# Opening of a fused FFT-and-gating kernel: loads of x and stores of turned weights moved into the next phase, bias rows sorted between its steps

## The chip, the cores and the metric

One core of one Trainium2 chip. The metric is device time in microseconds (us). Times from a trace are counted from the start of the profiled span, which is about 1.8 us shorter than the time of the same run. Engines: PE multiplies matrices, ACT (ScalarE) and DVE (VectorE) work on elements, POOL and SP here mostly issue DMAs; `bk` in a line is one of the banks that PE writes its results to. The granted clock is the share of PE's full clock that it was given, 1.00 for all of it; "half clock" below is a granted clock of 0.50.

## The reference

```python
X = fft(fft(x, axis=1), axis=2).real                # x: 8 x 3072 x 256
h = maximum(X @ w_in, 0)                            # 256 -> 1024
u, v = h[..., :512], h[..., 512:]
v_n = (v - mean(v)) / sqrt(var(v) + 1e-6)           # over the last axis
v_s = einsum('ts,bsd->btd', w_spatial, v_n) + b_spatial[None, :, None]
out = (u * v_s) @ w_out                             # 8 x 3072 x 256
```

`w_spatial` is 3072 x 3072. The kernel turns its rows on PE (transposes), keeps the turned rows on chip for the first batch and stores them in DRAM (`rawd`) for later batches. `b_spatial` has to be brought into the order in which the kernel makes its output rows.

## The kernel before

The opening makes the tables, folds x of batch 0 and turns the first three weight rows. Then comes V of batch 0: twelve tiles in a pipeline of steps t = 0, 1, 2, ... Each tile has two matmul halves, a root and a normalisation, so tile n has its root at step n + 2. ACT and DVE share this work, and the turning of weight rows 3 to 5 goes on in steps 1 to 9. After V the kernel goes through chunks of output until the end.

The bias rows go through this code. They are copied with strides into the fp32 columns 0 to 4607 of `regf`, a difference is added, and one store brings them to DRAM:

```python
def bias_sort():
    for src, so_, st, do_, ds in ((0, 0, 2, 0, 1152), (0, 1, 2, 2304, 1536),
                                  (1, 0, 2, 384, 1152), (1, 3, -2, 2688, 768)):
        DVE.tensor_copy(out=view(regf, do_, [[ds, 2], [1, 384]], 1),
                        in_=view(bsrc[src], so_, [[st, 2], [4, 384]], 1))
    rows = lambda k: view(regf, 384 * k, [[1152, 4], [1, 384]], 1)
    tt(DVE, rows(2), rows(0), rows(1), SUB)
    SP.dma_start(out=dram(bprm, 0, ...), in_=view(regf, 0, [[1, 4608]], 1))
```

`regf` is `reg` seen as fp32. Normalised V of batch 0 is written into `reg` from its first byte on: for tile 0 DVE writes the fp32 columns 0 to 255 and ACT the columns 3072 to 3327. Both lie within the sorted rows, so these must have been read out before V is written.

The opening and the loop of V, cut:

```python
prep_x(1, 0)                    # x of batch 1: SP loads it, POOL loads its mirror image
POOL.dma_start(out=wob, ...)    # w_out
...
prep_x(1, 1, homes[1])

def keep(i):                    # stores turned row i
    ACT.dma_start(out=dram(rawd, ...), in_=view(reg, ...))

def turning(i, on_dve=(1,)):    # three turn steps of row i; behind the last of them:
    def last(g=ts[-1]):
        g()
        keep(i)
        ...                     # the next weight loads by POOL
t0, t1, t2 = [turning(i, ()) for i in range(3)]
...
prep_x(1, 2, homes[2])
...
bias_sort()
load_bias(0)
for st in transform_steps(0, 0): st()
...
for t in range(len(pipes) + 5):
    if 5 <= t: first_products(*order[t - 5])
    for k in (3, 2, 1, 0):      # norm of tile t-3, root of t-2, second half of t-1, first half of t
        if 0 <= t - k < len(pipes): pipes[t - k][k]()
    for st in extra.get(t, ()): st()
    if 1 <= t < 10: ts[t - 1]()  # turning rows 3 to 5
    if 9 <= t < 17: us[t - 9]()
```

## Time and profile before

| | before |
|---|---|
| median of 6 runs (lowest to highest) | 1298.28 us (1296.81 to 1299.16) |
| span of the profiled run | 1295.2 us |
| PE busy | 96% of the span |
| ACT's first turn copy of V, and its first root | 48.28 and 50.61 us |
| ACT's first normalisation | 52.61 us |
| PE's last run of twelve matmuls of V's products before chunk 0 | 87.43 us |

PE is busy nearly throughout, so a change of the opening acts through *when* each later piece starts. I therefore follow one number through this text, the **lead**: how much earlier the same instruction starts than in the profiled run of the kernel before. The landmarks are ACT's root instructions (one for each tile of V) and, later, its copies of the output; at the end it is the difference of the spans.

### The profile page before, as it was taken

Reading aid. Unit: us, or ns where it says so; the run is one execution under the profiler, and the core shown is the slowest. Engines: PE = TensorE matmul, PEld = TensorE weight load, DVE = VectorE, ACT = ScalarE, POOL = GpSimd, SP = SyncE. Lnnn points to the kernel's source line nnn. Section 1 sums busy time; section 2 is a strip of 40 time slices with the busy share of each in tenths; the row PEclk is TensorE's granted clock in tenths of the full one; section 3 lists DMA queues with packets and bytes.
Section 4 is the critical chain, followed back from the end, with each engine's and each line's share of the span. In section 5 each row is a group of like instructions: output and inputs, shape, how many; then the busy total and the mean of one; then the engine's idle time right before and its main releaser. Section 6 shows DMA issues by size and latency. Waiting matters only on the chain.

```text
span 1295.2 us, 20931 instructions
## 1 busy us (share of the span) xinstructions
PE 1240.7 (96%) x8056; PEld 764.7 (59%) x8056; DVE 763.5 (59%) x1580; ACT 677.8 (52%) x1508; POOL 269.8 (21%) x318
## 2 busy tenths in 40 slices
PE   3689989999999999999999999999999999999998
PEld 2356555655666566665666666665666666666665
DVE  8677325446866846666555746666555744446333
ACT  8663767645554455555555455565555455551111
POOL 7101101002221222222121212222211112222222
PEclk9899999999999999999999999999999999999999
DMA  9949888576698878887788878887788778778885
GB/s 218 253 98 253 193 189 200 176 268 264 253 352 330 296 283 284 298 279 285 260 289 284 292 265 294 286 282 285 262 294 281 266 260 286 266 279 305 299 305 196
DMA packets 101442, 343.54 MB, mean 265 GB/s; under 512 B 7611, under 2 KB 57307, under 8 KB 77789
## 3 DMA queue, kind: packets, MB, share of 16 engines
q1 hardware_dynamic: 43902, 248.61, 54.0%
q0 software_dynamic: 25312, 49.55, 17.0%
q10 hardware_dynamic: 32128, 44.05, 9.6%
q8 instruction: 63, 1.03, 0.3%
q14 instruction: 37, 0.30, 0.1%
HBM read 300.46 MB, written 67.66 MB: 284 GB/s over the span
## 4 chain that ended last, share of the span: by engine, by line
PE 75%; issue 9%; ACT 6%; DVE 4%; POOL 3%; DMA 3%; ACTq 0%; POOLq 0%; DVEq 0%
PE bk L115 73%; POOL sumd L1011 2%; ACT reg L664 2%; PE bk L657 2%; DMA ovl<-in_moe_w_spatial_dram 1%; ACT junk L474 1%; ACT reg L488 1%; DMA sumd<-ovl 1%; DVE u L165 1%; DMA reg<-in_x_dram 1%; POOL reg L165 1%; DVE oto L165 1%; DVE xst L165 1%; DVE y L165 1%; ACT vt L466 0%
## 5 line engine op out<-in xcount | busy, mean ns | idle before, releaser
L115 PE MATMUL bk<-reg 128*128 128x384 bf16 (+1 forms) x5576 | 980.5, 326 | 8.3 <-ACT reg L664 3.6
L115 PEld LDWEIGHTS <-reg 128*128 128x128 bf16 x5576 | 541.9, 98 | 370.6 <-issue 16.1
L599 ACT COPY ost<-bk 128x512 f32<-128x512 f32 (+1 forms) x128 | 61.2, 480 | 251.6 <-PE bk L115 233.9
L165 POOL TENSOR_TENSOR p<-y,qt 128x384 f32<-128x384 f32 x48 | 62.7, 1307 | 545.0 <-DVE y L165 545.0
L488 ACT ACTIVATE reg<-vt,sm 128x512 bf16<-128x512 f32 x168 | 127.5, 806 | 46.7 <-DVE sm L165 44.4
L165 DVE TENSOR_TENSOR u<-y,u 128x384 bf16<-128x384 f32 x256 | 143.5, 561 | 10.1 <-ACT ost L599 0.5
L474 ACT ACTIVATE junk<-vt,sm 128x512 bf16<-128x512 f32 x168 | 121.3, 722 | 46.1 <-DVE sm L468 33.0
L165 DVE TENSOR_TENSOR y<-bk,bias 128x384 f32<-128x384 f32 x160 | 88.6, 554 | 80.9 <-PE bk L115 79.9
L115 PE MATMUL bk<-wob,u 128*128 128x256 bf16 x768 | 100.5, 273 | 0.2 <-ACT ost L599 0.2
L165 DVE TENSOR_TENSOR qt<-qt,bk 128x384 f32<-128x384 f32 x48 | 26.6, 554 | 124.0 <-PE bk L115 124.0
L580 ACT ACTIVATE u<-bk 128x384 bf16<-128x384 f32 x128 | 61.7, 482 | 67.1 <-PE bk L115 67.1
L574 ACT ACTIVATE u<-bk 128x384 bf16<-128x384 f32 x128 | 61.2, 478 | 50.8 <-PE bk L115 50.8
L115 PEld LDWEIGHTS <-u 128*128 128x128 bf16 x768 | 75.1, 98 | 19.6 <-DVE u L165 0.4
L165 POOL TENSOR_TENSOR qt<-y,qt 128x384 f32<-128x384 f32 x48 | 62.6, 1305 | 53.4 <-DVE y L165 53.0
L165 DVE TENSOR_TENSOR ovl<-reg 128x1536 bf16<-128x1536 bf16 x60 | 56.7, 952 | 23.6 <-DMA reg<-rawd 9.1
L453 ACT ACTIVATE vt<-bk 128x512 f32<-128x512 f32 x84 | 49.7, 591 | 35.1 <-PE bk L115 34.7
L468 DVE TENSOR_SCALAR sm<-sm 128x2 f32<-128x2 f32 x84 | 32.4, 386 | 55.5 <-ACT vt L466 54.5
L165 DVE TENSOR_TENSOR reg<-reg 128x3072 bf16<-128x3072 bf16 (+3 forms) x39 | 63.5, 1629 | 0.2
L466 ACT ACTIVATE vt<-bk 128x512 f32<-128x512 f32 x84 | 49.1, 584 | 27.8 <-PE bk L115 27.6
L1011 POOL DMA_DIRECT2D sumd<-ovl x60 | 32.6, 543 | 139.8 <-DVE ovl L165 129.1
L165 DVE TENSOR_TENSOR qt<-bias,bk 128x384 f32<-128x384 f32 x48 | 26.6, 553 | 59.5 <-PE bk L115 59.5
L165 POOL TENSOR_TENSOR p<-p,y 128x384 f32<-128x384 f32 x48 | 47.8, 996 | 59.2 <-DVE y L886 38.6
(144 smaller groups left out, 1258.1 us busy)
## 6 DMA issues: line engine op xcount, KB each, us to landing
reg<-sumd SPq DMA_DIRECT2D x120, 1152.0 KB
reg<-rawd SPq DMA_DIRECT2D x64, 1152.0 KB
out_dram<-ost ACTq DMA_DIRECT2D x64, 384.0 KB
sumd<-ovl POOLq DMA_DIRECT2D x60, 384.0 KB, 4.5
rawd<-reg ACTq DMA_DIRECT2D x24, 768.0 KB
bias<-bprm SPq DMA_DIRECT2D x32, 576.0 KB
ovl<-in_moe_w_spatial_dram POOLq DMA_DIRECT2D x34, 384.0 KB, 8.8
xst<-in_x_dram SPq DMA_DIRECT2D x20, 512.0 KB
```

What stands on the lines that cost most here:

```text
L115: PE.matmul(o, lhsT=l, rhs=r, start=start, stop=stop, skip_group_check=True)
L165: eng.tensor_tensor(out=o, in0=a, in1=b_, op=op)
L453: ACT.activation(out=v, in_=bk, func=AF.Relu, accum_out=sm[:, 0:1])
L466: ACT.activation(out=v, in_=bk, func=AF.Relu, accum_out=sm[:, 1:2])
L468: DVE.tensor_scalar(out=sm[:, 2:4], in0=sm[:, 0:2], scalar1=-1.0 / DH, scalar2=None, op0=MUL)
L474: ACT.activation(out=junk, in_=s["v%d" % i], func=AF.Square, bias=sm[:, 2 + i:3 + i], accum_out=sm[:, 4 + i:5 + i])
L488: ACT.activation(out=v_out(b, i, t), in_=v_in(b, s["v%d" % i]), func=AF.Identity, scale=sm[:, 6 + i:7 + i], bias=sm[:, 8 + i:9 + i])
L574: ACT.activation(out=u[:, jc, 0, :], in_=src, func=AF.Relu)
L580: ACT.activation(out=u[:, jc, 1, :], in_=src, func=AF.Relu)
L599: ACT.copy(out=s["o"][:, rs[0]:rs[0] + len(rs), :], in_=view(bk, 0, [[256, len(rs)], [1, 256]]))
L657: PE.transpose(bk[:, 128 * n:128 * n + 128], view(src, off, [[4, 128]]), idn)
L1011: POOL.dma_start(out=sumd[c, mi][:, 1536 * r:1536 * r + 1536], in_=o)
```

## The change

Its intent: take out of the opening what is not wanted there. x of batch 1 and the first stores go into the steps of V, where DMA is less busy, and the bias rows are sorted in gaps of DVE.

```diff
-        for src, so_, st, do_, ds in (...four copies...):
+        def copy(src, so_, st, do_, ds):
             DVE.tensor_copy(...)
-        rows = ...
-        tt(DVE, rows(2), rows(0), rows(1), SUB)
-        SP.dma_start(out=dram(bprm, ...), in_=view(regf, 0, [[1, 4608]], 1))
+        def diff():
+            rows = ...
+            tt(DVE, rows(2), rows(0), rows(1), SUB)
+            SP.dma_start(out=dram(bprm, ...), in_=view(regf, 0, [[1, 4608]], 1))
+            load_bias(0)
+        return [...the four copies...] + [diff]
...
-    prep_x(1, 0)
...
-    prep_x(1, 1, homes[1])
...
-    def turning(i, on_dve=(1,)):
+    def turning(i, on_dve=(1,), kept=True):
...
-            keep(i)
+            if kept:
+                keep(i)
...
-    t0, t1, t2 = [turning(i, ()) for i in range(3)]
+    t0, t1, t2 = [turning(i, (), False) for i in range(3)]
...
-    prep_x(1, 2, homes[2])
-    bias_sort()
-    load_bias(0)
...
-        ts += turning(i)
+        ts += turning(i, (1,), False)
+    later = {t: [] for t in range(len(pipes) + 5)}
+    for t, st in zip((0, 0, 1, 1, 2), bias_sort()):
+        later[t].append(st)
+    for j, t in enumerate((5, 8, 11)):
+        later[t].append(lambda j=j: prep_x(1, j, homes[j]))
+    for i, t in enumerate((7, 9, 10, 12, 14, 15)):
+        later[t].append(lambda i=i: keep(i))
...
-            for st in extra.get(t, ()):
+            for st in extra.get(t, []) + later[t]:
```

The stores of rows 3 to 5 move too.

More of the change, by code (lines that the diff above doesn't have):

```diff
@@ L378, in bias_sort @@
     def bias_sort():
-        for src, so_, st, do_, ds in ((0, 0, 2, 0, 1152), (0, 1, 2, 2304, 1536),
-                                      (1, 0, 2, 384, 1152), (1, 3, -2, 2688, 768)):
+        def copy(src, so_, st, do_, ds):
             DVE.tensor_copy(out=view(regf, do_, [[ds, 2], [1, 384]], 1),
                             in_=view(bsrc[src], so_, [[st, 2], [4, 384]], 1))
-        rows = lambda k: view(regf, 384 * k, [[1152, 4], [1, 384]], 1)
-        tt(DVE, rows(2), rows(0), rows(1), SUB)
-        SP.dma_start(out=dram(bprm, 0, [[4608, 1], [1, 4608]]),
-                     in_=view(regf, 0, [[1, 4608]], 1))
+        def diff():
+            rows = lambda k: view(regf, 384 * k, [[1152, 4], [1, 384]], 1)
+            tt(DVE, rows(2), rows(0), rows(1), SUB)
+            SP.dma_start(out=dram(bprm, 0, [[4608, 1], [1, 4608]]),
+                         in_=view(regf, 0, [[1, 4608]], 1))
+            load_bias(0)
+        return [lambda k=k: copy(*k) for k in (
+            (0, 0, 2, 0, 1152), (0, 1, 2, 2304, 1536),
+            (1, 0, 2, 384, 1152), (1, 3, -2, 2688, 768))] + [diff]
     def load_bias(n):
```

## The prediction

> **What bounds the kernel now.** I read the page first, then the chain of waits, the table of waits, the DMA queues in two windows and the timelines of ACT, DVE and SP in the opening.
>
> ```profile
> PE   3689989999999999999999999999999999999998
> PEclk9899999999999999999999999999999999999999
> ```
>
> One slice is 1295.2/40 = 32.4 us. PE is at nine tenths from the fourth slice on, so what the change can win lies in the first three slices (about 97 us), and after them a gain is only carried along. The change touches nothing later. The second slice (32 to 65 us) holds the loss; the chain of waits over 26 to 48 us names it:
>
> ```profile
> 27.81 19.30 DMA ovl<-in_moe_w_spatial_dram
> 47.11 0.05 issue
> 47.16 0.94 PE bk L657 x7
> ```
>
> The rows of weights for the fourth turn (i = 3) are requested at 27.81 and PE can turn them only at 47.16. The table of waits over 40 to 54 us gives what the engines lost (total, times, longest):
>
> ```profile
> ACT reg L664 <- PE bk L657: 5.9, 1, 5.9
> PE bk L657 <- DMA ovl<-in_moe_w_spatial_dram: 5.5, 1, 5.5
> ```
>
> Why that load takes 19.3 us: the same queue (q0, the software queue of POOL, which casts weights and mirrored x to bf16) carries 1.69 MB in 20 to 28 us, when it is nearly alone,
>
> ```profile
> DMA packets 635, 1.71 MB, mean 213 GB/s; under 512 B 76, under 2 KB 84, under 8 KB 634
> q0 software_dynamic: 614, 1.69, 107.8%
> ```
>
> and 0.32 MB in 34 to 42 us, an equally long window:
>
> ```profile
> q10 hardware_dynamic: 622, 1.81, 56.8%
> q0 software_dynamic: 621, 0.32, 28.4%
> q1 hardware_dynamic: 585, 0.58, 26.5%
> ```
>
> q10 is ACT's queue (the first three stores of turned rows, 3 x 786 KB), q1 is SP's (x of batch 1). With both running q0 falls from 211 to 40 KB/us. These two are what the change takes away.
>
> After 47 us the step from one tile of V to the next is bound by ACT (8.65 of 10 us busy in 60 to 70 us). Its timeline:
>
> ```profile
> 50.61 0.29 ACT L528 ACTIVATE reg<-reg,cst 128x2 f32<-128x2 f32 x1
> 52.61 0.81 ACT L544 ACTIVATE reg<-vt,reg 128x512 bf16<-128x512 f32 x1
> 53.33 0.28 ACT L528 ACTIVATE reg<-reg,cst 128x2 f32<-128x2 f32 x1
> 54.84 1.01 ACT L664 COPY reg<-bk 128x1024 bf16<-128x1024 bf16 x1
> 55.88 0.67 ACTq L762 DMA_DIRECT2D rawd<-reg  x1
> 56.59 0.81 ACT L544 ACTIVATE reg<-reg 128x512 bf16<-128x512 f32 x1 [0.74 <-DVE reg L637]
> ```
>
> L528 is the root of one tile, L544 the normalisation, L762 a store, whose issue alone holds ACT 0.67 us. The bias rows, on DVE and then SP:
>
> ```profile
> 35.23 3.13 DVE L382 COPY reg<-u 1x768 f32<-1x768 f32 x4
> 38.47 1.75 DVE L165 TENSOR_TENSOR reg<-reg 1x1536 f32<-1x1536 f32 x1
> ```
>
> ```profile
> 40.24 0.24 SPq L386 DMA_DIRECT2D bprm<-reg  x1
> 45.21 0.34 SPq L391 DMA_DIRECT2D bias<-bprm  x1
> ```
>
> Four copies and a difference hold DVE 4.9 us before the first tile of V; the rows go to DRAM (bprm) and SP sees the store landed 5.0 us later.
>
> **What the Trainium skill says.** "DMA: Bandwidth & Descriptors", section "Queues, rings and completion order": each DMA engine goes round the queues that have work, packet by packet. The trace agrees: q0 keeps its packet count (614 and 621 in equal windows) but moves a fifth of the bytes. The same page, "Anatomy of one DMA": a fixed cost of about 2 us, mostly the receipt of the write, before the semaphore fires. Here the bprm store took 5.0 us, as it stood behind x in q1: its one packet of 18,432 bytes started at 44.1 and took 0.70 us. A small SP load with free queues, at 97.97, landed at 99.3 (1.3 us). "TensorE: Matmul & The Clock Gate", "What's actually happening": PE's clock is halved after an idle window and freed by work. The trace agrees: the granted clock is 0.71 in 42 to 47 us and 0.51 in 47 to 51, so PE restarts at half speed.
>
> **The change part by part.**
> (a) Out of the opening go x of batch 1 (3 x 524 KB on q1; about 0.78 MB as written on q0) and three stores (2.36 MB on q10). q0 then keeps 211 KB/us. The load before the small weights still lands at 29.84; 262 KB of w_out take 1.2 us, the 393 KB in dispute 1.85: it lands near 33 instead of 47.1. PE wants it near 40, so the wait of 5.5 us is gone whole.
> (b) Two of the three store issues stood between ACT copies (0.44 us each with their gaps; the third fell into an idle stretch): the first A copy moves from 35.87 to about 35.1.
> (c) DVE copies the corner rows of A and B (L415 to L438) directly after B instead of after the bias rows (40.15). Following PE, ACT and DVE with the durations of before: B copy 36.95, half of the first tile 38.1, transform 1 done 38.9, second half 40.15, first half of tile 1 40.7, turn copy 40.7 to 41.7 (before: 48.28), table load to 43.0, first root at 43.0 (before 50.61). Lead here: 7.6 us.
> (d) The bias rows now sit in steps 0, 0, 1, 1, 2 of V. DVE: statistics to 38.8, two copies to 40.35, statistics 41.0, aggregates 41.3, statistics 42.0, two copies 43.55, reciprocal and product 43.9, statistics and aggregates of tile 1 44.9, of tile 2 45.55, difference 45.55 to 47.3. The copies hide; the difference does not quite, and something hangs on it. The normalisation writes V of batch 0 over the bytes where the sorted rows lie, so the first L541 of DVE and L544 of ACT must wait until the bprm store has been read out: the compiled order shows both waiting for the very semaphore of that store, in both kernels. Before, it had landed at 45.2, 7 us ahead of its use. Now it is issued at 47.3; q0's next four loads (issued 35.07 to 37.7) are done by about 46.7, so it meets free queues: 1.3 + 0.7 = 2.0 us, landed 49.4. ACT would be ready at 45.3: a new wait of about 4 us. The lead at the first L544 is 52.61 - 49.45 = 3.2 us.
> (e) From there ACT sets the pace. Stores of rows 3 and 4 (55.88, 66.20) leave steps 3 and 6, each +0.6: lead 4.2 by the root of step 4, 4.8 at step 7. Step 7 gets the first store instead: 4.2. Step 9 has one in both. Steps 10, 12, 14 and 15 have four more. In the trace PE takes over at 78.31, released by ACT, then runs without a break to chunk 0 (87.4); the store at step 10 stands before the two activations of step 11 that PE needs at 80.58: -0.6. At 12 and later ACT has gaps of 0.8 to 1.9 us and hides it.
> Sum at chunk 0: 4.2 - 0.6 = 3.6 us. Gross: 7.6 of lead plus 1.2, less 4 of new wait, less 1.2 of later stores.
>
> **The rivals.**
> 1. The new wait is short or hidden (the store lands at once, the difference comes earlier). For it: only 18 KB. Against it: the semaphore, and DVE's full list in steps 0 to 2. Then 6 to 8 us are won: 1291 to 1293.
> 2. The moved traffic takes the gain back later. Between 58 and 88 us come six stores (4.72 MB), x (1.57 + 0.78 MB) and six loads of weights (2.36 MB). At q0's 211 KB/us and the 365 KB/us of hardware queues alone that is 14.9 + 17.2 = 32 us of DMA in some 35 us from the first load at step 3. For it: hardware queues starve q0, as shown above. Against it: before, the DMA was at 0.03 of its share in 90 to 100 us, and a row loaded at step 3 to 9 is wanted only in chunk 0, up to 25 us later; x of batch 1 is first used at 92.5. If chunk 0 did wait: 0 to 2 us won, 1297 to 1299.
> 3. The bprm store meets traffic again and takes 4 to 5 us as before. Then the lead falls to about 1: 1298. Against it: q0 should be empty by 46.7, by a margin of only 0.6 us.
>
> **Range and chances.** 1299.2 - 3.6 = 1295.5. Three runs before spread over 1.7 us and the profiled one ran 1297.0, so the noise is near half of the effect. Rival 1 sets the low end at 1292, rivals 2 and 3 with the noise the high end at 1298.8. 2% is 26 us, more than the whole DMA wait and all of the bias work together: within 2% is almost sure (0.98), 0.01 either side.
>
> **What would show it.** Right: no wait of PE for the weights load near 41 to 47; the first turn copy of V near 40.7; one idle stretch of 3 to 5 us on ACT and DVE just before the first normalisation, ended by the bprm store, with the root of tile 1 near 50.2; a longer DMA-busy stretch from 58 to about 88; PE in chunk 0 near 84, with nothing lost to 250 us. Wrong: ACT normalising at 45 to 46 (rival 1); PE, or ACT's turn copies, idle on a DMA in 84 to 110 us (rival 2); or a span below 1291, where the carried lead grew in chunks 1 to 3, which I take as fixed.

## More of the kernel before

Apart from what the prediction shows, two lines are needed for comparison. They are a table of windows. The columns are: window and its length, then busy us (and instructions) of PE, PE's weight loads, DVE, ACT and POOL, then PE's granted clock, the share of the DMA engines and GB/s. Before:

```profile
42.00:47.00 5.00, 0.00 (x0) 0.00 (x0) 1.42 (x4) 0.39 (x1) 0.00 (x0) 0.71 1.20 250
47.00:51.00 4.00, 3.84 (x17) 2.18 (x18) 0.07 (x1) 2.69 (x4) 0.00 (x0) 0.51 1.08 263
```

PE does nothing from 42 to 47 us and then runs at half clock to 51 us.

## The result and the profile after

| | before | after |
|---|---|---|
| median of 6 runs | 1298.28 us | 1294.15 us |
| lowest to highest | 1296.81 to 1299.16 | 1293.41 to 1295.54 |
| span of the profiled run | 1295.2 | 1291.6 |

The ratio is 0.9969, with a 95% interval of 0.9957 to 0.9982. Ratios here are the mean time of one kernel's fast runs over that of the other's fast runs of the same rounds, so they are not quite the ratios of the quoted medians. By the 2% limit the two are the same. The change wins some 4 us, 0.3%, and the interval leaves no doubt that it wins something. The page's PE rows of the kernel after:

```profile
PE   3799989899999999999999999999999999999998
PEclk9899999999999999999999999999999999999999
```

In place of 6 and 8 the second and third slices have 7 and 9: the loss in the second is smaller but still there. The landmarks, beside what the prediction said:

| us from the start | before | predicted | after |
|---|---|---|---|
| weights for the fourth turn landed | 47.1 | near 33 | 32.84 |
| ACT's first turn copy of V | 48.28 | 40.7 | 41.01 |
| first root | 50.61 | 43.0 | 43.34 |
| difference of the bias rows starts on DVE | 38.47 | 45.55 | 45.56 |
| store of the bias rows issued | 40.24 | 47.3 | 47.35 |
| ... landed | about 45.2 | 49.4 | 49.06 |
| ACT's first normalisation | 52.61 | 49.45 | 49.16 |
| last twelve products before chunk 0 on PE (ten of them are in the trace of after) | 87.43 | near 84 | 83.51 |

The chain of waits of the kernel after (start, length, what) no longer holds a weights load. It holds the bias rows:

```profile
45.64 1.66 DVE reg L165
47.35 1.71 DMA bprm<-reg
49.16 0.59 ACT reg L550
...
51.99 4.47 PE bk L115 x13
```

ACT's timeline shows the wait and what came after it (start, length, engine, line, operation, output from input, and in brackets the idle time before it with what ended it; L544 of before is L550 here, as the file is six lines longer at that place, and L522 is a half of a tile, L534 a root, L766 the issue of a store):

```profile
49.16 0.81 ACT L550 ACTIVATE reg<-vt,reg 128x512 bf16<-128x512 f32 x1 [3.81 <-DMA bprm<-reg]
...
54.58 0.48 ACT L419 CAST A<-bk 128x384 bf16<-128x384 f32 x1 [0.67 <-PE bk L115]
56.49 0.48 ACT L441 CAST B<-bk 128x384 bf16<-128x384 f32 x1 [1.44 <-PE bk L115]
57.22 1.01 ACT L670 COPY reg<-bk 128x1024 bf16<-128x1024 bf16 x1 [0.24 <-PE bk L663]
...
64.56 0.59 ACT L522 ACTIVATE vt<-bk 128x512 f32<-128x512 f32 x1
64.94 0.40 ACTq L766 DMA_DIRECT2D rawd<-reg  x1
65.04 0.60 ACT L522 ACTIVATE vt<-bk 128x512 f32<-128x512 f32 x1
```

The first line is the predicted wait. Of the next three, two were **not** predicted: ACT waits for PE for 0.67 and 1.44 us, 2.11 us in all. (The third, 0.24, is shorter than the 0.31 that the kernel before has at that copy, 59.62.) The last three show a moved store: its issue lies inside ACT's own work and leaves no gap. The windows of the kernel after say why PE was late:

```profile
42.00:47.00 5.00, 3.36 (x26) 1.99 (x24) 4.84 (x10) 3.33 (x7) 0.00 (x0) 1.00 0.61 119
47.00:51.00 4.00, 0.47 (x5) 0.35 (x6) 2.08 (x6) 1.84 (x4) 0.00 (x0) 0.88 0.22 78
51.00:57.00 6.00, 5.60 (x22) 2.90 (x23) 4.30 (x14) 3.86 (x8) 2.52 (x4) 0.51 1.02 308
```

While ACT and DVE wait for the store of 18 KB, PE has nothing to do from 47 to 51 us (0.47 us busy), and from 51 to 57 its granted clock is 0.51. It is busy 5.6 of 6 us there, with 22 matmuls. PE's timeline in that stretch:

```profile
51.18 0.59 PE L115 MATMUL bk<-w2d,B 128*128 128x512 bf16 x1 [2.77 <-ACT vt L522]
...
52.41 0.52 PE L115 MATMUL bk<-tabc,fOC 128*128 128x384 bf16 x1
52.73 0.52 PE L115 MATMUL bk<-tabs,fOC 128*128 128x384 bf16 x1
```

The starts are 0.32 us apart; the same kind of matmul at full clock, at 42.15 and 42.31 in this trace, starts 0.16 us apart. The halved period of before (44.1 to 50.9 in the clock records) has not gone away. It has moved to 50.1 to 56.9 (e4 and e12 below take the idle time away and with it the low clock).

So the lead runs like this, root by root: 7.3 at the first root, 3.4 at the second (behind the new wait), 4.7 at the third, 2.4 at the fourth (half clock), 3.2 at the sixth, 3.9 at the ninth, and 3.9 at the first output copy at 118 us of before. It stays 3.9 to 361 us, then falls to 3.6 and ends there.

### The profile page after: what moved, and what is told of

The parts are those of the page before. It is cut to its first block, busy times and chain, and to the rows that moved or that the text cites. A ratio compares the mean times of both kernels' runs of the same rounds, so it can differ in the third digit from the quotient of the medians.

```text
span 1291.6 us, 20870 instructions
## 1 busy us (share of the span) xinstructions
PE 1237.1 (96%) x7995; PEld 764.7 (59%) x8056; DVE 764.6 (59%) x1580; ACT 677.4 (52%) x1508; POOL 268.1 (21%) x318
## 4 chain that ended last, share of the span: by engine, by line
PE 80%; ACT 6%; issue 6%; DVE 5%; POOL 1%; DMA 1%; ACTq 0%; POOLq 0%; DVEq 0%; SPq 0%
PE bk L115 79%; ACT reg L670 2%; PE bk L663 2%; ACT junk L480 1%; POOL sumd L1021 1%; DVE oto L165 1%; ACT reg L494 1%; DMA sumd<-ovl 1%; DVE u L165 1%; DVE y L165 1%; DVE xst L165 1%; ACT vt L472 0%; DVE ovl L165 0%; DVE reg L524 0%; DVE sm L474 0%
## 5 line engine op out<-in xcount | busy, mean ns | idle before, releaser
L494 ACT ACTIVATE reg<-vt,sm 128x512 bf16<-128x512 f32 x168 | 127.6, 806 | 47.1 <-DVE sm L165 44.8
L580 ACT ACTIVATE u<-bk 128x384 bf16<-128x384 f32 x128 | 61.2, 478 | 50.1 <-PE bk L115 50.1
L165 DVE TENSOR_TENSOR ovl<-reg 128x1536 bf16<-128x1536 bf16 x60 | 56.7, 953 | 23.4 <-DMA reg<-rawd 9.3
L165 DVE TENSOR_TENSOR reg<-reg 128x3072 bf16<-128x3072 bf16 (+3 forms) x39 | 63.5, 1629 | 0.1
```

The source lines that it names most:

```text
L165: eng.tensor_tensor(out=o, in0=a, in1=b_, op=op)
L494: ACT.activation(out=v_out(b, i, t), in_=v_in(b, s["v%d" % i]), func=AF.Identity, scale=sm[:, 6 + i:7 + i], bias=sm[:, 8 + i:9 + i])
L580: ACT.activation(out=u[:, jc, 0, :], in_=src, func=AF.Relu)
```

## The experiments

My theory after the result: the change is a sum of a gain (x and stores out of the opening, and stores apart from their own copies) of about 8 us and a loss (bias rows spread out) of about 4 us. The loss has two parts, the wait for the bias store's read-out and PE's halved clock that follows from it. The rivals: the traffic that was moved costs the missing time later; and the issues of moved stores on ACT cost it.

Twelve runs were made, in groups that shared a chip and the runs of the kernel before. All gave correct results. The table of leads, in us, against the profiled run of the kernel before:

| run | root 1 | root 2 | root 3 | root 4 | root 6 | root 9 | output copy at 118 | at 230 | at the end |
|---|---|---|---|---|---|---|---|---|---|
| after | 7.3 | 3.4 | 4.7 | 2.4 | 3.2 | 3.9 | 3.9 | 3.9 | 3.6 |
| e1_bias_only | 0.7 | -3.3 | -3.0 | -4.3 | -4.3 | -4.3 | -4.3 | -5.9 | -6.9 |
| e2_x_and_stores | 5.9 | 6.1 | 6.8 | 6.8 | 7.6 | 8.3 | 8.3 | 8.3 | 8.3 |
| e3_bias_early | 7.5 | 6.2 | 7.4 | 7.4 | 8.1 | 8.9 | 8.9 | 8.9 | 8.7 |
| e4_warm_pe | 7.8 | 4.0 | 5.2 | 5.2 | 6.0 | 6.7 | 6.7 | 5.3 | 4.1 |
| e5_other_bytes | 7.1 | 7.3 | 6.6 | 5.4 | 6.2 | 7.0 | 6.9 | 5.2 | 4.8 |
| e6_early_other | 7.4 | 7.5 | 8.2 | 8.2 | 9.0 | 9.7 | 9.7 | 9.7 | 10.0 |
| e7_early_keep_own | 7.1 | 5.8 | 6.1 | 6.1 | 6.1 | 6.1 | 6.1 | 6.1 | 5.8 |
| e8_early_six_issues | 8.0 | 6.1 | 7.4 | 6.3 | 7.0 | 7.5 | 7.4 | 5.8 | 5.4 |
| e9_x_only | 5.3 | 5.4 | 5.3 | 5.3 | 5.3 | 5.3 | 5.3 | 3.9 | 3.5 |
| e10_stores_only | 5.9 | 6.0 | 6.7 | 6.7 | 7.5 | 8.3 | 8.2 | 6.9 | 5.2 |
| e11_after_again | 7.4 | 3.5 | 4.8 | 2.5 | 3.3 | 4.1 | 4.0 | 4.0 | 3.0 |
| e12_warm_pe_again | 7.4 | 3.6 | 4.8 | 4.8 | 5.6 | 6.4 | 6.3 | 4.6 | 3.7 |

A trace is one run, and the profiled run of before (1296.98 us) is a fast one among its kind. So read the leads for *where* time goes, and the medians for how much. Edits below are against the kernel after.

### e1_bias_only: the bias part alone

```diff
+    prep_x(1, 0)              # the three x loads and the stores back where they were
     POOL.dma_start(out=wob, ...)
...
-    t0, t1, t2 = [turning(i, (), False) for i in range(3)]
+    t0, t1, t2 = [turning(i, ()) for i in range(3)]
...
-    for j, t in enumerate((5, 8, 11)): later[t].append(... prep_x ...)
-    for i, t in enumerate((7, 9, 10, 12, 14, 15)): later[t].append(... keep ...)
```

> The third part of the change alone: bias rows between the steps of V, x and stores where they were before. My theory: PE's wait for the weights load stays (first turn of V near 47), the difference now ends near 54.5, the bprm store meets a busy q0 and lands near 57, so the first normalisation slips from 52.6 to about 57: slower than before by 3 to 5 us, 1301 to 1303. Rival (spreading the rows is itself a gain of DVE time before V): 1296 to 1298.

Measured: 1302.32 us (1300.98 to 1303.89, 4 runs) against 1297.88; ratio 1.0031 [1.0018, 1.0044]. Alone, spreading the bias rows is a loss of 4.4 us by the medians. ACT's timeline of this run:

```profile
55.95 0.81 ACT L550 ACTIVATE reg<-vt,reg 128x512 bf16<-128x512 f32 x1 [3.98 <-DMA bprm<-reg]
```

The wait is the one of the kernel after, in the same place (before: 52.61, no wait), and the clock records show half clock again behind it, from 56.7 to 63.5.

### e2_x_and_stores: the other part alone

```diff
     for st in t1[2:] + t2:
         st()
+    for st in bias_sort():
+        st()
...
-    for t, st in zip((0, 0, 1, 1, 2), bias_sort()):
-        later[t].append(st)
```

> The first two parts without the third: bias rows sorted in one block before V, as before. My theory: the block delays the first statistics by about 2.5 us, but the bprm store lands near 43 and no one waits for it; first normalisation near 46 instead of 49.2, PE not idle long enough to lose its clock: 2 to 4 us faster than the changed kernel, 1290 to 1292. Rival (the spreading pays for itself, as the change intends): slower than the changed kernel, 1295 to 1297.

Measured: 1291.25 us (1288.73 to 1292.72, 5 runs); ratio 0.9945 [0.9932, 0.9958]. The bias store is issued at 40.32 and lands at 45.98, and ACT normalises at 46.56 without a wait. The clock stays full until the very end. At the first output copy the leads of e1 and e2 add up to -4.3 + 8.3 = 4.0, and the kernel after has 3.9: the two parts add up there, and the change as a whole is less than its better half. The medians are too coarse to confirm the sum: -4.4 + 6.6 = 2.2 us against 4.1 measured, with runs of e1 that spread over 2.9 us and runs of e2 over 4.0.

### e3_bias_early: half of the copies before the first transform

```diff
-    for st in transform_steps(0, 0):
+    bs = bias_sort()
+    for st in bs[:2] + transform_steps(0, 0):
         st()
...
-    for t, st in zip((0, 0, 1, 1, 2), bias_sort()):
-        later[t].append(st)
+    later[0] += bs[2:]
```

> The changed kernel with two of the copies placed in DVE's idle time before the first transform and the other two and the difference in step 0. My theory: difference done near 42.3, bprm landed near 44.2, first normalisation near 45.4 with no wait, no slow clock after it: 4 to 6 us faster than the changed kernel, 1288 to 1290. Rival (ACT or PE sets the pace anyway and the wait of 3.8 us was only slack): 1293 to 1295.

Measured: 1290.86 us (1288.26 to 1293.78, 6 runs); ratio 0.9945 [0.9931, 0.9959]. I had expected 1288 to 1290 and no wait, but a wait remained. The store is issued 5.2 us earlier, at 42.16, but it lands at 46.36, only 2.7 us earlier: it takes 4.2 us instead of 1.71, while the weights loads are still running (its packet started at 45.31 and took 0.7 us; the last load landed at 45.83). ACT's idle time before the normalisation falls from 3.81 to 1.26 us. The profile puts that rest down to a DVE copy, which ended at the same time as the store landed, so it does not tell the two apart; e6 does. No half clock appears. The profiled run was the fastest of the six, so its lead of 8.9 overstates the kernel; the median gain is 7.0.

### e4_warm_pe: PE kept busy during the wait

```diff
+    def heat(n):
+        for _ in range(n):
+            mm(banks[3], idn, w1[:, DH:DFF], True, True)   # result never read
...
+        if t == 3: heat(6)
         if 1 <= t < 10:
             ts[t - 1]()
+        if t == 3: heat(12)
```

> The changed kernel with 18 extra matmuls of 128x512 into an unused bank in step 3, so that PE is not idle while ACT waits for the bprm store; that wait itself stays. My theory: granted clock 1.00 in 51 to 57 us, matmuls of the transform in step 4 start 0.16 us apart instead of 0.32, ACT does not wait for PE there: about 2 us faster than the changed kernel, 1291.5 to 1293. Rival (the halved clock is hidden behind ACT): same as the changed kernel, 1294.

Measured: 1293.19 us (1292.62 to 1293.96, 5 runs); ratio 0.996 [0.9948, 0.9972]. This leaves ACT's wait as it is (3.81 us) and takes away the low clock alone: it is 1.00 from 51 to 57 us, and the lead from the third root to the fourth stays at 5.2 instead of falling by 2.3. At the first output copy this run leads the one of the kernel after by 2.8 us. But then 3.4 us at half clock appear at 175 us and take 1.4 us, and the medians differ by 1 us only. e12 repeats this against e11.

### e5_other_bytes: the sorted rows where the first normalisation does not write

The rows lie at `regf` 256 and 3328 on instead, in two halves with two differences and two stores, at the same (late) step.

```diff
-            (0, 0, 2, 0, 1152), (0, 1, 2, 2304, 1536),
-            (1, 0, 2, 384, 1152), (1, 3, -2, 2688, 768))] + [diff]
+            (0, 0, 2, 256, 1152), (0, 1, 2, 3328, 1536),
+            (1, 0, 2, 640, 1152), (1, 3, -2, 3712, 768))] + [diff]
...
+            for h in range(2):      # difference and store, each half by itself
+                rows = lambda k: view(regf, 256 + 3072 * h + 384 * k, [[1152, 2], [1, 384]], 1)
```

> The changed kernel with the sorted rows in other bytes of the same buffer (two halves, stored by two transfers), which the first tile of V does not overwrite; the difference still comes late, in step 2. My theory: the wait of 3.8 us of ACT before the first normalisation is due to the overlap of bytes alone; it goes, the second tile waits for little or nothing, no slow clock: 3 to 5 us faster than the changed kernel, 1289 to 1291. Rival (DVE is late in any case because of the difference of 1.7 us): at most 1 us faster, 1293 to 1294.

Measured: 1292.48 us (1291.88 to 1293.37, 5 runs) against 1298.34; ratio 0.9956 [0.9943, 0.9969]. The wait for the store is gone, and with it the fall of the lead at the second root (7.3 in place of 3.4). So the overlap of bytes is what made ACT wait. But the run missed my expectation of 1289 to 1291, and its ACT timeline shows why:

```profile
48.64 0.60 ACT L523 ACTIVATE vt<-bk 128x512 f32<-128x512 f32 x1 [1.77 <-PE bk L664]
```

ACT now waits 1.77 us for PE's transposes. They wait for a bank that DVE copies out, and that copy (47.42 us) stands behind the two differences (45.69 to 47.4 us) on DVE. PE idles again and the clock is halved from 49.9 to 53.3. A late difference costs by holding DVE, whatever bytes it writes.

### e6_early_other: both remedies together

This is e3 with the rows of e5.

```diff
+    bs = bias_sort()
+    for st in bs[:2] + transform_steps(0, 0):     # as in e3
...
+            (0, 0, 2, 256, 1152), (0, 1, 2, 3328, 1536),    # as in e5
```

> Both cures at once: the early sorting of e3 and the other bytes of e5. In e3 the first normalisation still came at 46.4, just when the store landed (46.4). My theory: first normalisation near 45.3, about 1 us faster than e3: 1289 to 1290. Rival (after e3 DVE or ACT alone set the pace): the same as e3, 1290 to 1291.

Measured: 1288.72 us (1287.03 to 1291.89, 6 runs) against 1298.34; ratio 0.9926 [0.9915, 0.9938]. It beats both kernels, and its interval lies wholly below those of the kernel after and of e5. ACT's first normalisation and root of the next tile:

```profile
45.15 0.84 ACT L551 ACTIVATE reg<-vt,reg 128x512 bf16<-128x512 f32 x1
45.87 0.31 ACT L535 ACTIVATE reg<-reg,cst 128x2 f32<-128x2 f32 x1
47.01 0.60 ACT L523 ACTIVATE vt<-bk 128x512 f32<-128x512 f32 x1 [0.34 <-PE bk L664]
```

The normalisation starts at 45.15 with no wait, although the rows of this run land only at 46.28 and the DVE copy that stood in question in e3 runs here from 45.77 to 46.46. So what ACT waited for in e3 was the store. ACT has no idle time longer than 0.34 us from there to the third root, PE's clock stays full, and the lead of 7.4 won in the opening is carried on and grows to 9.7. (This profile too is of the fastest run.)

### e7_early_keep_own: stores of rows 3 to 5 behind their own copies again

This is e3, with the three stores back at steps 3, 6 and 9.

```diff
-        ts += turning(i, (1,), False)
+        ts += turning(i)
...
-    for i, t in enumerate((7, 9, 10, 12, 14, 15)):
+    for i, t in enumerate((7, 9, 10)):
```

> e3 with the stores of rows 3, 4 and 5 put back directly behind their own copies (steps 3, 6, 9), as in the kernel before; the first three stay moved. My theory: a store directly behind the copy that it reads waits for that copy to end, so nothing of ACT overlaps its issue, 0.6 to 0.8 us each; one that stands later is issued while the engine works on and costs nothing: 1.5 to 2.2 us slower than e3, 1292 to 1293, all of it in the roots of steps 4, 7 and 10. Rival (the prediction's: each issue costs ACT 0.6 wherever it stands, only those at steps 12 to 15 are hidden): at most 1.2 us slower.

Measured: 1291.2 us (1290.92 to 1292.5, 5 runs); ratio 0.9948 [0.9936, 0.9959]. The totals do not tell it from e3, whose runs scatter over 5.5 us, and the expected 1292 to 1293 was missed. The traces tell them apart. ACT's timeline of e7:

```profile
48.71 1.00 ACT L670 COPY reg<-bk 128x1024 bf16<-128x1024 bf16 x1
49.74 0.66 ACTq L766 DMA_DIRECT2D rawd<-reg  x1
50.46 0.81 ACT L550 ACTIVATE reg<-reg 128x512 bf16<-128x512 f32 x1 [0.75 <-DVE reg L643]
```

The store waits for the copy whose result it reads, its issue begins when that has ended, and nothing of ACT runs meanwhile: 0.75 us idle. (DVE L643 is named as what ended it, but it is the issue that fills the gap.) The same occurs at 60.07 (0.68) and 69.15 (0.66). In the kernel after, the store at 64.94 was shown above with no gap. From the start of the copy to the start of ACT's next instruction it takes 1.75 us here (48.71 to 50.46) and 0.89 in e3 (48.31 to 49.20); at the two other places 1.69 and 1.67 against 0.90 and 0.89. That is 2.4 us in all, and so is the difference of the leads: from the second root on, e3 grows from 6.2 to 8.9 and e7 from 5.8 to 6.1.

### e8_early_six_issues: six more issues on ACT

This is e3 with six extra stores of 32 KB of a constant tile, in steps 3 to 8.

```diff
+    for t in range(3, 9):
+        later[t].append(lambda t=t: ACT.dma_start(out=spare[t - 3], in_=idn))
```

> e3 with six more stores of 32 KB issued by ACT in steps 3 to 8 from data that was ready long before. My theory: they overlap ACT's own work and cost nothing: same as e3, 1290 to 1291.5. Rival (each issue costs ACT 0.4 to 0.67 wherever it stands): 2.4 to 4 us slower, 1293 to 1295.

Measured: 1291.59 us (1290.19 to 1292.15, 5 runs); ratio 0.9945 [0.9933, 0.9957]. Each issue lasts 0.33 to 0.48 us and overlaps ACT's work. Four of them come after the fourth root. From there to the first output copy the lead grows by 1.2 (6.25 to 7.43) against 1.5 in e3, so these four cost 0.3 us together; 0.24 of it is an idle gap of ACT behind the one issue (61.51) that followed another store within half a microsecond. The loss between the third and fourth root (1.1) is a half clock from 48.4 to 51.8 us, as PE was late in this run.

### e9_x_only: x moved, stores as before, bias in one block

```diff
-    t0, t1, t2 = [turning(i, (), False) for i in range(3)]
+    t0, t1, t2 = [turning(i, ()) for i in range(3)]      # stores at their old places
...
+    for st in bias_sort(): st()                          # as in e2
...
-    for i, t in enumerate((7, 9, 10, 12, 14, 15)): ...keep...
```

> The kernel before with x of batch 1 moved alone; the first stores and the bias rows as before. My theory: the software queue has only w_out (done by 31) ahead of the weights in dispute, and the stores begin at 31 to 33, so that load lands at 33 to 36 and PE's wait is gone; bias rows in one block, no wait for the bprm store: 5 to 7 us faster than before. Rival (the stores alone starve the software queue): PE still waits 2 to 4 us.

Measured: 1293.34 us (1292.54 to 1294.38, 4 runs) against 1298.62; ratio 0.9958 [0.9944, 0.9973]. The load in dispute lands at 33.68 and PE no longer waits for it. The lead is 5.3 at the first root and stays there: with the stores behind their own copies nothing is gained in steps 3, 6 and 9.

### e10_stores_only: stores moved, x as before, bias in one block

```diff
+    prep_x(1, 0)                                         # x at its old places
     POOL.dma_start(out=wob, ...)
...
+    for st in bias_sort(): st()                          # as in e2
...
-    for j, t in enumerate((5, 8, 11)): ...prep_x...
```

> The kernel before with the first three stores moved alone; x and the bias rows as before. My theory: x is the larger part of it: 0.78 MB of it stands in the software queue itself and 1.57 MB in SP's queue beside it, so the load in dispute lands near 38 to 42 and PE waits little or not at all at 41: 3 to 6 us faster than before, less than with x alone. Rival (x alone starves the queue as both do): lands near 45, 1 to 2 us faster.

Measured: 1290.83 us (1290.47 to 1291.8, 4 runs); ratio 0.9938 [0.9921, 0.9954]. I had taken x for the larger part, and that was wrong. The load lands at 39.45, late but before PE asks for it (41.66), so stores alone remove that wait as well. The leads are those of e2, step by step, up to the first output copy: once the stores are moved, moving x as well gains nothing there. The DMA queues of this run in 34 to 42 us (packets, MB, share of 16 engines):

```profile
q0 software_dynamic: 1412, 1.18, 91.8%
q1 hardware_dynamic: 689, 0.67, 30.7%
```

With x beside it the weights' queue q0 still moves 1.18 MB in this window, against 0.32 MB before, when it had x and the stores beside it. It takes both to hold the load up so far that PE waits, but they act differently. Two loads of before that stood in q0 ahead of the weights in dispute, issued at 22.04 and 26.10 (KB each, us from issue to landing):

```profile
wob<-in_moe_w_out_dram POOLq DMA_DIRECT2D x1, 256.0 KB, 17.6
reg<-in_x_dram POOLq DMA_DIRECT2D x1, 256.0 KB, 19.3
```

The second, a mirror image of x of batch 1, lands at 45.37, and the weights behind it land 1.7 us later, at 47.11. In e10 the same two land at 37.29 and 39.45. In e9 no x stands in q0: w_out lands at 31.54 and the weights at 33.68. So x delays the weights by standing ahead of them in their own queue, and the stores make that queue slower.

### e11_after_again and e12_warm_pe_again: the clock once more, on one chip

The kernel after and e4's kernel, unchanged.

```diff
 (e11: no edit; e12: the edit of e4)
```

> The changed kernel again, on the same chip and in the same rounds as e12, since e4's gain of 1.0 us came from different rounds than the changed kernel's own. My theory: 1293.5 to 1295, with halved clock in 50 to 57 us in its profile.

> e4 again beside e11. My theory: 1 to 2.5 us below e11, the trace with full clock in 50 to 57 us and a lead at chunk 0 about 2.5 us larger than e11's. Rival (the halved clock only shifts waiting and the 1.0 us was chance): equal to e11 within 0.5 us.

Measured: e11 1293.96 us (1293.35 to 1295.12, 9 runs), ratio 0.997 [0.9961, 0.998]; e12 1293.32 us (1291.94 to 1295.45, 5 runs), ratio 0.9968 [0.9955, 0.998]. The totals cannot be told apart, so the 1 to 2.5 us that I expected between them was missed. The traces repeat what e4 showed: with the extra matmuls the lead stays at 4.8 from the third root to the fourth, without them it falls from 4.8 to 2.5, and at the first output copy it is 6.3 against 4.0. Then e12 loses 1.7 us in one place. The window 175 to 180 us of e12, and the idle time of PE before it:

```profile
175.00:180.00 5.00, 4.10 (x19) 2.23 (x20) 0.83 (x2) 0.84 (x1) 0.00 (x0) 0.66 0.95 257
```

```profile
175.90 0.41 PE L663 MATMUL bk<-idn,reg 128*128 128x128 bf16 x4 [2.56 <-ACT reg L670]
```

And the same two views of e11:

```profile
175.00:180.00 5.00, 2.42 (x24) 1.58 (x22) 0.86 (x2) 3.15 (x6) 0.00 (x0) 1.00 0.90 200
```

```profile
178.20 0.42 PE L663 MATMUL bk<-idn,reg 128*128 128x128 bf16 x4 [2.56 <-ACT reg L670]
```

Both have the same gap of 2.56 us on PE, and so, at its own time, has each of the fourteen traces (2.56 or 2.57 us; before at 182.2, e2 at 173.96). After it the clock falls for 3.4 us in e12 and not in e11. Of the thirteen traces besides the one of before (two of the kernels are there twice), seven show such a low period of 3.4 us between 174 and 190 us, and each costs 1.3 to 1.7 us. Whether it comes is thus not decided by the kernel's own gaps alone.

The clock records show what decides. In every trace each recorded period of full or low clock but the last is a whole multiple of 3.413 us (326 of them are the 1112.7 us behind e12's low period). So the clock changes on a grid of windows of 3.413 us, and this grid lies differently against the kernel from run to run. Laid over PE's busy time between 40 and 1280 us, it separates the cases: of the windows at full clock, the fourteen that a fall follows were busy for 14 to 39%, and all others, in all fourteen traces, for 42% or more. In e12 the window from 173.1 to 176.5 holds the whole gap (173.3 to 175.9) and was busy for 25%. In e11 a border lies at 176.2, inside the gap (175.6 to 178.2), and the emptier of its two windows was busy for 42%. The busy shares are those of a profile whose matmul ends are modelled, so 39 and 42% are no exact limit.

What the extra matmuls win in total is left open: 2.3 us in the trace up to 118 us, and 0.6 us, within the noise, at the end. The chance of a low period is not the whole of that noise: two runs of e12 had a mean clock of 1.000 and took 1291.94 and 1293.29 us, and three of e3's at 0.999 took 1288.26, 1291.7 and 1293.49. What else moves single runs was not looked into.

## Why the prediction was right, and where its terms were off

**The class, the range and the median** came out: 1295.5 predicted, 1294.15 measured. Part of that is luck: two errors of about 2 us, shown under (e), cancelled.

**(a) The weights load** was right: near 33 predicted, 32.84 measured, no wait of PE. The prediction gave the credit to both x and stores together. e9 and e10 show that either alone removes the wait. One of its readings does not bear what it puts on it: that q0 kept its packet count and moved a fifth of the bytes (614 packets with 1.69 MB, 621 with 0.32) says that its packets had become smaller, 0.5 in place of 2.8 KB. What speaks for the queues taking turns is that in 34 to 42 us three of them moved nearly the same number of packets: 622, 621 and 585.

**(b), (c) The opening** was right within 0.4 us (first root 43.34 against 43.0, lead 7.3 against 7.6).

**(d) The bias rows** were right in mechanism and size: difference at 45.56, store 1.71 us, wait 3.81 us against "about 4". e5 shows the mechanism (other bytes, no such wait) and e1 what it costs by itself. The prediction's reason for the 5.0 us of the store before, x in the same queue, is not needed: with x moved away it took 5.7 us in e2 and 5.0 in e9, again beside running weights loads.

**(e) The steps after it** are where the terms were mis-sized, and the errors cancelled:

| term | predicted | measured in the trace |
|---|---|---|
| lead behind the first normalisation | 3.2 | 3.4 |
| up to the root of step 4 (third root; the text's 4.2 is 0.4 more than its own terms give) | +1.0 | +1.2 |
| PE's clock behind the wait | nothing | -2.3 |
| store left step 6 | +0.6 | +0.8 |
| store made at step 7 | -0.6 | 0 |
| step 9 ("one in both") | 0 | +0.8 |
| store made at step 10 | -0.6 | 0 |
| lead at chunk 0 | 3.6 | 3.9 |

The prediction priced every store issue on ACT alike, at 0.6 us. What costs is an issue directly behind the copy that it reads (e7: 0.8 to 0.9 us each, of which 0.66 to 0.75 is idle). A store of rows that were finished steps ago is issued while ACT works on: the three at 64.94, 70.62 and 73.25 cost nothing in the lead, and in e8 four extra ones cost 0.3 us together. So step 9 has a store in both kernels, but only before is it the dear kind. That is 2.0 us better than predicted over steps 7, 9 and 10. Against it stands the halved clock, 2.3 us, which the prediction had seen in the kernel before and explained from the idle time of PE. It then put an idle stretch of the same kind behind the new wait, and did not ask what PE's clock would do there. e4 and e12 remove that loss in the trace. So the term of the sum that was missing is PE's clock, and the one that was mis-sized is the price of a moved store.

**The rivals.** Rival 1 (no or little wait) did not occur in the kernel after; e6 is the kernel in which it does, and it ran at 1288.7. Rival 2 (moved traffic takes the gain back; the 365 KB/us of its sum stands in no view on record) did not occur: in the lead nothing is lost between the ninth root and 361 us, and e2, with the same moved traffic, keeps its 8.3 to the end. One detail was placed wrongly: x was to come at steps 5, 8 and 11, yet SP issued it at 49.48 to 51, right behind the bias load (49.07), since SP has nothing else to wait for. Rival 3 (the bias store meets traffic) did not occur in the kernel after, as the store was issued 1.9 us after the last weights load had landed (45.44). In e3, where it was issued at 42.16, it did: 4.2 us.

**Where the expected gain went.** x and stores alone are worth 6.6 us by the medians (e2), the whole change 4.1. (The stores alone bring as much: 7.8 us in e10, in other rounds, with the leads of e2.) The difference went into spreading the bias rows: late enough on DVE and over bytes that V wants.

## What to carry to other kernels

Before filling gaps with "free" work, look at what its result's bytes and its engine are wanted for next: here the sorting of 18 KB of bias rows held the first root back by 1.3 us in its old place (44.68 in e2, 43.34 in after), and in its new place it cost 3.8 us of waiting and 2.3 us of half clock. Price a DMA issue by what stands in front of it: directly behind the producer on the same engine it cost ACT 0.8 us, a few steps later it was nearly free. And when a wait idles PE, price PE's half clock behind it too, and expect single runs to differ by about 1.5 us through one low period of the clock.

## What the Trainium skill lacked or had wrong

- "DMA: Bandwidth & Descriptors", "Anatomy of one DMA — SWDGE (gpsimd) path", gives a fixed cost of about 2 us, mostly the write's receipt, for DMAs that POOL issues. This store of 18 KB went through SP's hardware queue. It took 1.71 us when the other queues were empty, which is near that figure, but 4.2 us in e3, 5.7 us in e2 and 5.0 us before, beside running loads. The page has no figure for that waiting, most of which lies before the packet starts (e3: issued at 42.16, started at 45.31).
- The same page, "Queues, rings and completion order", says that an engine goes round its queues by packet. It does not say what that means in bytes: in 34 to 42 us of before three queues moved 621, 622 and 585 packets, but 0.32, 1.81 and 0.58 MB.
- "TensorE: Matmul & The Clock Gate", "What's actually happening", has the half clock after an idle window of about 3.4 us, free-running and different from run to run. The runs agree with the length and the free running: all recorded periods but the last of each trace are multiples of 3.413 us. They do not agree that the window has to be idle: in the fourteen windows before a fall PE was busy for 14 to 39%. The page has no figure for that share. Nor does it warn that the loss, here 1.3 to 2.3 us for each low period or 0.1 to 0.2% of the span, is as large as the effects looked for in a tuned kernel.
- No page that I read has the cost of a DMA issue on ACT by its place. (The DMA page has one figure for an issue, 512 sequencer cycles for "previous generations", in its part on trn3 B0.) Here it was 0.66 to 0.75 us of idle ACT directly behind the copy that it reads (e7), and no gap for the three issues of 0.37 to 0.40 us inside other work (64.94, 70.62 and 73.25 in after).
